# A second output bank for the second-layer products of three early two-unit slots, in a linear-attention and mixture-of-experts kernel

## The chip, the core and the metric

The kernel runs on one core of one Trainium2 chip. The metric is device time in microseconds (us) of one execution. The engines are named as in the profile: PE (TensorE, the matrix engine), PEld (its weight loads), DVE (VectorE), ACT (ScalarE), POOL (GpSimd) and SP (SyncE, which issues most of the DMA transfers). A matrix product is written into PSUM, a small memory of eight banks of 128 partitions by 512 float32 numbers, and DVE or ACT reads it from there.

## The reference

There are two parts in a row. The first is attention without softmax, for 8 batches of 8 heads with 576 tokens of 64 numbers; the second sends each of the 4608 tokens (512 numbers: 8 heads of 64) through one of 8 two-layer networks (experts).

```python
def phi(x):
    proj = np.einsum('bhsd,df->bhsf', x, w_phi)
    proj = proj - np.max(np.abs(proj), axis=-1, keepdims=True)
    return np.concatenate([np.exp(proj), np.exp(-proj)], axis=-1)
q_p, k_p = (phi(q), phi(k))
kv = np.einsum('bhsf,bhsd->bhfd', k_p, v)
z = np.sum(k_p, axis=2)
num = np.einsum('bhsf,bhfd->bhsd', q_p, kv)
den = np.einsum('bhsf,bhf->bhs', q_p, z)[..., None] + 1e-06
return (num / den).astype(np.float32)
...
logits = np.einsum('bsd,de->bse', x, w_gate)
...
    h = np.maximum(x[b, s] @ w1[e], 0.0)
    out[b, s] = p[e] * (h @ w2[e])
```

The expert `e` of a token is the largest of its eight logits, or, where a second gate says so, the expert of the token before it; `p` is the softmax of the logits.

## The kernel before

**Attention.** Work goes through the batches in four pairs. For each chunk of 128 tokens PE projects (`pj`), turns (`qt`), accumulates the key-value sums (`kvp`) and multiplies (`nm`). Its PSUM pools are `psf` (five banks), `pskv` (one bank, `kvp`) and `psb` (two banks, tag `nm`). The gate of each pair of batches gives every token an expert, and POOL writes the tokens with indirect DMAs into a list for each expert (`lst`).

**Units and slots.** In the second part the work is cut into units of 128 tokens of one expert. A slot takes one or more units through one expert's weights. A slot needs eight weight blocks of 128x1024, four for each layer. A block comes by DMA as `wraw`, ACT casts it to `whi` (line 861) and DVE takes the rest, `wlo` (line 862); every product is made of three matmuls (lines 928 to 930: `whi` and `wlo` with the high and the low part of the other operand). `layer1` writes four PSUM tiles `l1` (pool `psl`, two banks); ACT makes `hh` of each (line 963) and DVE `hl` (line 964), and the third and fourth tiles wait until the first and second have been read. `layer2` adds up 24 matmuls of 512 columns for each unit `k` in one tile `l2`; DVE scales it to `y` (line 1015), and POOL writes `y` to the output (line 1018).

**The three early slots.** Three slots of two units each run ahead of the main list of slots, right behind attention, by the call in line 144. At that time the pool `psf` has been closed and its banks belong to `psm4` (one buffer for `l2`, one for the transposes `tr`) and `psl`; `pskv` and `psb` are still open, since the last gate and the planning of the main slots use them (`pst`, tile `pt`, tag `nm`). Both units of an early slot have their `l2` in the one bank of `psm4`. Behind the third early slot `back.close()` and `open_rest` give the place of `pskv`, `psb` and attention's SBUF tiles to the pools `psr` (two buffers each for `tr` and `l2`) and `ml1` (more `wraw` buffers).

**Planning.** Between them the early slots carry the plan of the main slots: `plan_main` counts units (line 641, PE, tile `pt`; then a chain of small DVE operations from line 643), reads the token lists with indirect DMAs (`lr`, line 619), and turns them on PE (line 632, tile `pt`); DVE makes of it the token numbers `p_tokm`, with which POOL gathers the tokens (`xg`, line 889). The two steps of `plan_main` are called inside `layer2` of the first and of the second early slot, behind the first three matmuls of its second unit.

**What sets the order.** Each engine runs its instructions in one fixed order. The order is not that of the code: outside attention's loop a scheduler sets it when the kernel is built, from its own estimates of when operands and buffers are there. So a changed buffer can move instructions on every engine.

In the listings below tiles carry numbers. `l_6256` and `l_6310` are the two `l2` tiles of the first early slot, `l_6654` and `l_6684` those of the second, `l_6831` and `l_6861` those of the third; `l_6723`, `l_6750`, `l_6777` and `l_6804` are the four `l1` tiles of the third early slot, and `l_7003` and `l_7045` the first two of the first main slot.

Of the kernel before, what the change touches and what calls it, by code (L numbers as in the profile page):

```python
# [6 lines left out]
F32 = mybir.dt.float32  # L7
# [10 lines left out]
DM, E, FF = 512, 8, 1024  # L18
# [31 lines left out]
class Kernel:  # L50
# [944 lines left out]
    def layer2(self, s, gi, between, held=None):  # L995
        tc, dve, pool = self.tc, self.dve, self.pool
        hh, hl = s["h"][gi]
        u0 = s["u"] + sum(s["n"][:gi])
        for k in range(s["n"][gi]):
            self.l2n = getattr(self, "l2n", 0) + 1  # L1000
            p = self.psr if hasattr(self, "psr") and self.l2n % 3 else self.psm4
            t = p.tile([128, DM], F32, name="l2")
            o = slice(k * 128, k * 128 + 128)
            for f in range(8):
                c = slice((f % 2) * DM, (f % 2) * DM + DM)
                self.both(s, 4 + f // 2, t, hh[:, f, o], hl[:, f, o], c, f == 0, f == 7)
                if f in (0, 2) and between:
                    between.pop(0)()
                if f % 2 and gi == len(s["n"]) - 1 and k == s["n"][gi] - 1:
                    self.used(1)  # L1010
                elif f % 2:
                    self.spare()
            y = self.mx2.tile([128, DM], F32, name="yl", bufs=1) if held is not None else self.mx2.tile([128, DM], F32, name="y")
            u = u0 + k
            dve.tensor_scalar_mul(y, t, s["prob"][:, u:u + 1])  # L1015

            def put(y=y, at=s["tok"][:, u:u + 1]):
                ins = pool.indirect_dma_start(self.A["out"], bass.IndirectOffsetOnAxis(at, 0), y, None,  # L1018
                                              bounds_check=NT - 1, oob_is_err=False)
                tc.declare_no_dep(ins.ins, group="outs", reason="each token is written once")  # L1020
                tc.add_to_no_dep_group("outs", ins.ins)
            if held is None:
                put()
            else:
                held.append(put)
# [162 lines left out]
```

## Time and profile before

| | |
|---|---|
| median of 3 runs | 796.64 us (796.41 to 796.94) |
| the profiled execution: time, span | 796.07 us, 794.0 us |
| PE busy | 767.4 us (97%) |
| PEld busy | 676.2 us (85%) |
| DVE busy | 511.2 us (64%) |
| ACT busy | 401.9 us (51%) |
| POOL busy | 158.0 us (20%) |
| mean granted clock of TensorE | 0.994 of full speed |

The span is the stretch from the first to the last recorded instruction; some 2 us of the execution lie around it. Matmuls overlap, so that a busy PE is not yet a PE at its peak. The three early slots run from about 317 to 396 us of the span.

### The profile page before, as it was taken

The numbers are of one execution on the slowest core, as the hardware profiler recorded it, in microseconds if no ns is written. First come the engines' busy times: TensorE is split into PE (matmuls) and PEld (weight loads), VectorE is DVE, ScalarE is ACT, GpSimd is POOL, SyncE is SP. The second block draws the span as 40 slices with busy tenths as digits, with TensorE's granted clock in tenths as the row PEclk, the third lists the DMA queues.
The fourth block names the chain that finished last, engine by engine and source line by source line (L and its number), as shares of the span: only waits on it lengthen the run. The fifth ranks groups of instructions, "written<-read, shape, count | busy, mean of one in ns | idle before, by whom it ended". The sixth has DMA issues, their size and how long they took to land.

```text
span 794.0 us, 23193 instructions
## 1 busy us (share of the span) xinstructions
PE 767.4 (97%) x9674; PEld 676.2 (85%) x9674; DVE 511.2 (64%) x939; ACT 401.9 (51%) x708; POOL 158.0 (20%) x166
## 2 busy tenths in 40 slices
PE   6999999999999999999899999999999999999993
PEld 5899988988888989988798997698988987689882
DVE  4677798789878886985742225544866824768621
ACT  4666566666687665544531114433745713757410
POOL 0000001200275132166121102102321311110100
PEclk9999999999999999999999999999999999999997
DMA  7655454454687721747922695733966679959300
GB/s 200 195 163 155 116 146 128 135 139 122 172 264 208 223 77 42 225 148 277 333 83 88 261 347 180 258 120 114 362 204 201 244 262 410 358 188 321 111 27 14
DMA packets 77227, 151.29 MB, mean 191 GB/s; under 512 B 8524, under 2 KB 50828, under 8 KB 77078
## 3 DMA queue, kind: packets, MB, share of 16 engines
q1 hardware_dynamic: 67424, 127.33, 49.6%
q0 software_dynamic: 7424, 20.08, 7.1%
q10 hardware_dynamic: 2272, 2.37, 0.9%
q8 instruction: 77, 1.26, 0.7%
q14 instruction: 30, 0.25, 0.1%
HBM read 128.21 MB, written 22.06 MB: 189 GB/s over the span
## 4 chain that ended last, share of the span: by engine, by line
PE 84%; DVE 5%; DMA 4%; issue 2%; ACT 1%; SPq 1%; another core or an unknown queue 0%; POOLq 0%; POOL 0%; DVEq 0%
PE l L928 15%; PE l L930 15%; PE l L929 15%; PE kvp L255 9%; PE nm L314 9%; PE pj L213 9%; PE qt L233 4%; PE l L941 4%; DMA wraw<-in_w1h 3%; PE tr L914 2%; DVE m L216 1%; PE nm L293 1%; DVE sb L218 1%; PE nm L281 1%; PE tr L980 1%
## 5 line engine op out<-in xcount | busy, mean ns | idle before, releaser
L861 ACT CAST whi<-wraw 128x1024 fp32r<-128x1024 f32 x136 | 142.2, 1048 | 155.9 <-PE l L930 68.9
L862 DVE TENSOR_TENSOR wlo<-wraw,whi 128x1024 fp32r<-128x1024 f32 x128 | 156.2, 1222 | 75.4 <-ACT whi L861 73.7
L928 PE MATMUL l<-xhi,whi 128*128 128x256 f32 x512 | 146.2, 285 | 1.0 <-DVE hl L964 1.0
L930 PE MATMUL l<-xhi,wlo 128*128 128x256 f32 x512 | 143.7, 281 | 0.0
L929 PE MATMUL l<-xlo,whi 128*128 128x256 f32 x512 | 143.6, 281 | 0.0
L216 DVE TENSOR_REDUCE m<-pj 128x8 f32<-128x1024 f32 x72 | 87.8, 1220 | 47.4 <-PE pj L213 46.8
L928 PE MATMUL l<-whi,hh 128*128 128x512 f32 x288 | 114.5, 398 | 2.7 <-DVE y L1015 1.7
L930 PE MATMUL l<-whi,hl 128*128 128x512 f32 x288 | 113.2, 393 | 0.6 <-DVE hl L964 0.6
L929 PE MATMUL l<-wlo,hh 128*128 128x512 f32 x288 | 112.7, 391 | 0.0
L236 ACT ACTIVATE qp<-qt 128x512 f32<-128x512 f32 x144 | 84.7, 604 | 52.5 <-PE qt L233 52.0
L222 ACT ACTIVATE kp<-sb 128x512 f32<-128x512 f32 x144 | 82.8, 622 | 50.4 <-DVE sb L218 44.1
L928 PEld LDWEIGHTS l<-xhi,whi 128*128 128x128 f32 x512 | 96.8, 189 | 3.5 <-DVE hl L964 1.5
L929 PEld LDWEIGHTS l<-xlo,whi 128*128 128x128 f32 x512 | 96.8, 189 | 0.4
L930 PEld LDWEIGHTS l<-xhi,wlo 128*128 128x128 f32 x512 | 96.9, 189 | 0.1
L213 PE MATMUL pj<-first,kq 64*128 64x128 f32 x1152 | 85.5, 289 | 6.8 <-DMA kq<-in_kqT 6.8
L218 DVE TENSOR_TENSOR sb<-pj,m 128x1024 f32<-128x1024 f32 x72 | 88.1, 1224 | 4.0
L1018 POOL DMA_INDIRECT out<-y,p_tokm x31 | 39.2, 1263 | 244.2 <-DVE y L1015 243.6
L314 PE MATMUL nm<-kvs,qp 128*64 128x74 f32 x2304 | 86.7, 228 | 0.3
L213 PEld LDWEIGHTS pj<-first,kq 64*128 64x128 f32 x1152 | 71.5, 191 | 12.1 <-issue 4.6
L314 PEld LDWEIGHTS nm<-kvs,qp 128*64 128x64 f32 x2304 | 79.3, 136 | 1.4 <-ACT kvs L295 0.5
L255 PE MATMUL kvp<-v,kp 128*64 128x65 f32 x2048 | 77.3, 225 | 0.0
L255 PEld LDWEIGHTS kvp<-v,kp 128*64 128x64 f32 x2048 | 67.7, 139 | 5.9 <-issue 5.7
(229 smaller groups left out, 1028.1 us busy)
## 6 DMA issues: line engine op xcount, KB each, us to landing
wraw<-in_w1h SPq DMA_DIRECT2D x68, 512.0 KB, 5.3
wraw<-in_w2h SPq DMA_DIRECT2D x68, 512.0 KB, 5.1
kq<-in_kqT SPq DMA_DIRECT2D x47, 384.0 KB, 3.9
v<-in_va SPq DMA_DIRECT2D x48, 195.0 KB, 3.7
xs<-xo SPq DMA_DIRECT2D x48, 128.0 KB, 2.4
whi<-in_w1h SPq DMA_DIRECT2D x8, 512.0 KB, 4.3
wlo<-in_w1h SPq DMA_DIRECT2D x8, 512.0 KB, 5.0
whi<-in_w2h SPq DMA_DIRECT2D x8, 512.0 KB, 10.4
```

What stands on the lines that cost most here:

```text
L213: self.last_pe = self.pe.matmul(t[:, h, i % 2, j, :], kq[r, j, s], self.w2[r], start=True, stop=True)
L216: dve.tensor_reduce(m, f, AX.X, ALU.max, apply_absolute_value=True)
L218: self.last_dve = dve.tensor_sub(sb.rearrange("p h c j f -> p (h c j) f"), f, m.unsqueeze(2).broadcast_to([128, 8, 128]))
L222: self.last_act = act.activation(kp[:, :, :, sg, :].rearrange("p c h f -> p h c f"), sb[:, :, :, 0], AF.Exp, scale=1.0 - 2 * sg)
L236: self.act.activation(qp[:, sg], t, AF.Exp, scale=1.0 - 2 * sg)
L255: self.pe.matmul(self.kvp[r, sg, h], self.ch[i]["kp"][:, h, sg, r], self.v(i, b)[:, h], start=first and n < 2, stop=last and n >= 6)
L314: self.pe.matmul(e["t"][r, c - c0, h, :], self.ch[i]["qp"][:, sg, h, q0 + r.start:q0 + r.stop], kvs[:, sg, h, :], start=sg == 0, stop=sg == 1)
L861: self.act.copy(hi, raw)
L862: (low or self.dve).tensor_sub(lo, raw, hi.bitcast(F32))
L928: mm(o, ah, bh, start=first, stop=False)
L929: mm(o, ah, bl, start=False, stop=False)
L930: self.last_pe = mm(o, al, bh, start=False, stop=last)
```

## The change

In `layer2`, as long as `psr` does not exist (that is, in the early slots alone), the first unit (`k` is 0) keeps the bank of `psm4`, and the second unit takes one of the two banks of `psb` by the tag `nm`. In the main slots the choice between `psr` and `psm4` stays.

```diff
             self.l2n = getattr(self, "l2n", 0) + 1
-            p = self.psr if hasattr(self, "psr") and self.l2n % 3 else self.psm4
-            t = p.tile([128, DM], F32, name="l2")
+            if hasattr(self, "psr"):
+                p, kw = self.psr if self.l2n % 3 else self.psm4, {}
+            else:
+
+                p, kw = (self.psb, dict(tag="nm")) if k else (self.psm4, {})
+            t = p.tile([128, DM], F32, name="l2", **kw)
             o = slice(k * 128, k * 128 + 128)
```

No instruction is added or taken away. The scheduler answers with other orders. On PE, in the second early slot, this is what stands before around the first matmuls of the second unit (`l_6684`), and behind them the transposes of the token lists:

```order
L930 MATMUL l_6723<-xhi,wlo 128x256
L928 MATMUL l_6723<-xhi,whi 128x256
L929 MATMUL l_6723<-xlo,whi 128x256
L928 MATMUL l_6684<-whi,hh 128x512
L929 MATMUL l_6684<-wlo,hh 128x512
L930 MATMUL l_6684<-whi,hl 128x512
L632 MATMUL pt<-first,lr 128x40 x2
```

The same place in the changed kernel:

```order
L928 MATMUL l_6654<-whi,hh 128x512
L929 MATMUL l_6654<-wlo,hh 128x512
L930 MATMUL l_6654<-whi,hl 128x512
L928 MATMUL l_6684<-whi,hh 128x512
L929 MATMUL l_6684<-wlo,hh 128x512
L930 MATMUL l_6684<-whi,hl 128x512
L632 MATMUL pt<-first,lr 128x40 x2
```

Eleven matmuls of the next slot's first layer (`l_6723`) stood between the two units; they now come behind the second unit. In the first early slot eight such matmuls move in the same way.

On ACT, in the third early slot, this stands before, from the first weight cast for the first main slot (`whi_6955`) on:

```order
L861 CAST whi_6955<-wraw_6953 128x1024
L861 CAST whi_6961<-wraw_6959 128x1024
L963 ACTIVATE hh_6721<-l1_6723 128x512
L861 CAST whi_6967<-wraw_6965 128x1024
L861 CAST whi_6973<-wraw_6971 128x1024
L963 ACTIVATE hh_6721<-l1_6750 128x512
L861 CAST whi_6979<-wraw_6977 128x1024
L861 CAST whi_6985<-wraw_6983 128x1024
L963 ACTIVATE hh_6721<-l1_6777 128x512
```

The same place in the changed kernel:

```order
L861 CAST whi_6955<-wraw_6953 128x1024
L861 CAST whi_6961<-wraw_6959 128x1024
L861 CAST whi_6967<-wraw_6965 128x1024
L963 ACTIVATE hh_6721<-l1_6723 128x512
L861 CAST whi_6973<-wraw_6971 128x1024
L861 CAST whi_6979<-wraw_6977 128x1024
L963 ACTIVATE hh_6721<-l1_6750 128x512
L861 CAST whi_6985<-wraw_6983 128x1024
L861 CAST whi_6991<-wraw_6989 128x1024
L963 ACTIVATE hh_6721<-l1_6777 128x512
```

Each of the three `hh` now stands behind one weight cast more; on DVE `hl` and `wlo` have changed places in the same way.

On PE, at the end of the third early slot, the first unit is followed by the second, where eight transposes of the first main slot's tokens stood between:

```order
 L929 MATMUL l_6831<-wlo,hh 128x512
 L930 MATMUL l_6831<-whi,hl 128x512
-L914 MATMUL tr<-first,xg 128x128 x8
 L928 MATMUL l_6861<-whi,hh 128x512
 L929 MATMUL l_6861<-wlo,hh 128x512
```

Behind the second unit the first main slot begins:

```order
 L929 MATMUL l_6861<-wlo,hh 128x512
 L930 MATMUL l_6861<-whi,hl 128x512
-L914 MATMUL tr<-first,xg 128x128 x8
+L914 MATMUL tr<-first,xg 128x128 x14
 L928 MATMUL l_7003<-xhi,whi 128x256
+L928 MATMUL l_7045<-xhi,whi 128x256
+L914 MATMUL tr<-first,xg 128x128 x6
 L929 MATMUL l_7003<-xlo,whi 128x256
 L930 MATMUL l_7003<-xhi,wlo 128x256
```

Twenty transposes now stand there, where eight stood: the eight that were between the units, the eight that were here, and four (of a later tile) from further on. Four of the twenty write into a buffer of `psr` that lies on the bank of `l_6861`, and so wait for its `y`; the last four wait for the `xlo` that DVE makes of those. ACT casts all four token tiles (`xhi`) behind the fifth weight cast there, where two came ahead of four of the casts.

## Rows read from the trace of the kernel before

**Rows 1.** The page, busy time of each engine

```profile
PE 767.4 (97%) x9674; PEld 676.2 (85%) x9674; DVE 511.2 (64%) x939; ACT 401.9 (51%) x708; POOL 158.0 (20%) x166
```

**Rows 2.** Windows 397 to 781 us: sum of busy times (x)

```profile
sum 384.00, PE 383.99 PEld 333.37 DVE 198.62 ACT 160.10 POOL 67.04; mean PE 96.00 PEld 83.34 DVE 49.65 ACT 40.03 POOL 16.76
```

**Rows 3.** Waits of PE, 310 to 445 us: total, times, longest

```profile
PE l L928 <- DVE y L1015: 1.7, 2, 1.2
PE l L928 <- DVE hl L964: 1.0, 1, 1.0
PE l L928 <- DVE p_rim L607: 0.9, 1, 0.9
```

**Rows 4.** Timeline of PE, first and second slot: start, us

```profile
338.22 0.21 PE L641 MATMUL pt<-cnt,consts 128*36 128x8 bf16 x2
...
361.29 0.28 PE L928 MATMUL l<-xhi,whi 128*128 128x256 f32 x1
...
363.96 0.50 PE L928 MATMUL l<-whi,hh 128*128 128x512 f32 x1 [1.21 <-DVE y L1015]
...
364.85 0.41 PE L632 MATMUL pt<-first,lr 40*128 40x40 f32 x2
...
370.13 0.28 PE L930 MATMUL l<-xhi,wlo 128*128 128x256 f32 x1
```

**Rows 5.** Timeline of DVE, first and second slot

```profile
338.44 0.23 DVE L643 TENSOR_SCALAR p_um<-pt 36x8 int32<-36x8 f32 x2 [1.17 <-PE pt L641]
...
362.02 1.22 DVE L862 TENSOR_TENSOR wlo<-wraw,whi 128x1024 fp32r<-128x1024 f32 x1 [0.87 <-ACT whi L861]
363.16 0.74 DVE L1015 TENSOR_SCALAR y<-l,p_probe 128x512 f32<-128x512 f32 x1
```

**Rows 6.** Waits of SP's DMA queue, 356 to 366 us

```profile
SPq L851 <- PE pt L632: 2.0, 1, 2.0
SPq L851 <- DVE wlo L862: 1.2, 1, 1.2
SPq L851 <- DMA lr<-lst,p_rim: 1.0, 1, 1.0
```

**Rows 7.** The list's DMAs, 330 to 372 us: issue to landing

```profile
DMA to landing us min/median/max: 2.1/2.3/6.0
```

**Rows 8.** Timeline of PE, third slot and what follows

```profile
378.43 0.38 PE L928 MATMUL l<-xhi,whi 128*128 128x256 f32 x1 [0.95 <-DVE hl L964]
...
381.40 0.39 PE L928 MATMUL l<-whi,hh 128*128 128x512 f32 x1
...
387.15 0.50 PE L930 MATMUL l<-whi,hl 128*128 128x512 f32 x1 [0.63 <-DVE hl L964]
...
388.19 1.03 PE L914 MATMUL tr<-first,xg 128*128 128x128 f32 x8
389.75 0.51 PE L928 MATMUL l<-whi,hh 128*128 128x512 f32 x1 [0.53 <-DVE y L1015]
...
395.42 1.03 PE L914 MATMUL tr<-first,xg 128*128 128x128 f32 x8
396.20 0.37 PE L928 MATMUL l<-xhi,whi 128*128 128x256 f32 x1
```

**Rows 9.** Timeline of ACT, third slot

```profile
378.34 1.05 ACT L861 CAST whi<-wraw 128x1024 fp32r<-128x1024 f32 x1 [1.34 <-DMA wraw<-in_w2h]
...
395.66 1.05 ACT L861 CAST whi<-wraw 128x1024 fp32r<-128x1024 f32 x1 [0.33 <-PE l L930]
396.61 1.06 ACT L923 CAST xhi<-tr 128x512 fp32r<-128x512 f32 x2
```

**Rows 10.** Timeline of DVE, third slot

```profile
377.68 0.69 DVE L964 SCALAR_TENSOR_TENSOR hl<-l,hh 128x512 fp32r<-128x512 f32 x1
...
396.51 0.75 DVE L1015 TENSOR_SCALAR y<-l,p_probf 128x512 f32<-128x512 f32 x1
397.22 1.29 DVE L924 TENSOR_TENSOR xlo<-tr,xhi 128x512 fp32r<-128x512 f32 x2
```

## The prediction

> **What bounds the kernel now.** I read the page's busy times first: PE has work for 97% of the span [rows 1], so time is won only where PE stands still. The windows behind the early slots show PE without a gap up to its end: 383.99 of 384 us [rows 2]. What moves the first main slot's start therefore moves the end by as much, and all that counts is when PE begins there, at 396.20 in the trace [rows 8]. Third, the waits of PE around the early slots. They are few, and they name what the change is about: twice 1.7 us together for `y`, once 0.9 us [rows 3]. That one is put down to `p_rim`, but its matmul is the first of `l_6654`, which needs the bank that `y` of the unit before it still reads; `p_rim` only stands next to `y` on DVE. The timelines give the two of `y`: 1.21 us at 363.96 [rows 4] and 0.53 us at 389.75 [rows 8]. So 0.90 + 1.21 + 0.53 = 2.64 us of PE's time lie in waits for one bank, and 1.6 us more in waits for `hl` in the third slot [rows 8]. I make the sum against the profiled execution's 796.07 us; the median of the runs is 0.57 us above it, and I put the difference found on top of the median.
>
> **What the change does, part by part.** It adds and removes no instruction. It removes waits and moves work, so I follow PE from slot to slot.
>
> *First early slot.* The eight matmuls that PE does before while `y` is made cover that wait entirely; nothing is won on PE. But the counting matmuls (`pt`, line 641) come earlier, as eight matmuls no longer stand ahead of them. DVE waits 1.17 us for them and starts its planning chain at 338.44 [rows 5]. In the new order the second of the two has to wait until DVE has read the first, so not all of that is won: I take 0.7 us for the chain. Then the 0.90 us wait goes too, and PE reaches the second unit of the second slot, `l_6684`, some 0.5 us ahead of 361.29 [rows 4], say at 360.8.
>
> *Second early slot.* Before, PE does eleven matmuls from 361.29, waits for `y` until 363.96, does three of `l_6684`, and then the transposes of the list (line 632) at 364.85 [rows 4]. `y` was late because DVE had a `wlo` of 1.22 us ahead of it [rows 5]. Now the three matmuls run at once and the transposes are due at 361.5. They need the list read (`lr`), though. SP's queue waits for three things in a row ahead of its next load: 1.0 for the list read, 1.2 for `wlo`, 2.0 for the transposes [rows 6]. Counted back from the end of the transposes (364.85 + 0.41, about 365.25), the list was there at about 362.05. POOL issues it behind the list's writes, which the change doesn't move; so I leave that time as it is, and the new wait is the list read, about 0.6 us. The transposes then run at 362.15, which is 2.7 us earlier, and SP's loads of the first main slot's weights follow them.
>
> PE itself wins less there. Twenty-one matmuls at 0.23 us and then the eleven bring it to where it was at 370.13 [rows 4] by about 368.8.
>
> *Third early slot.* What PE waits for here is `hl` of the second `l1` tile, until 378.43 [rows 8]; DVE makes it at 377.68 [rows 10]. In the new order one weight block more stands ahead of it on ACT and on DVE: the one that is cast at 378.34, when its DMA had landed [rows 9]. If its landing came 2.7 us earlier, as the loads' start does, the cast would begin at 375.6 and take 1.05, `wlo` 1.22 behind it, `hl` 0.69: 378.5, and no time is won. If POOL's gathers, which start less than SP's loads do ahead of time, leave the loads more of the DMA engines, I put the landing 4 us earlier at most, and `hl` is there at 377.3. So the last `l1` tile begins at 377.3 to 378.5 against 378.43; I take the middle, **-0.5 us**.
>
> From there to the end of the second unit the trace has 395.42 - 378.43 = 16.99 us [rows 8]. The last `l1` tile takes 381.40 - 378.43 = 2.97 of it; a unit without waits takes 395.42 - 389.75 = 5.67, with a slow first matmul behind its wait, and I take 5.6. Without the two waits and without the transposes between: 2.97 + 2 x 5.6 = 14.17. That is **-2.8 us**. I cost the wait for `hl` inside the unit (0.63 at 387.15 [rows 8]) at nothing, since the loads ahead of it are at least 2.7 us earlier; if that cover is gone it is back whole.
>
> *Start of the main slots.* Call the end of `l_6861` T (before: 395.42). Before, eight transposes follow and the first main matmul stands at T + 0.78 [rows 8]. Now the first tile's tokens are still to be turned, and one of the buffers is the bank that `y` of `l_6861` reads. The trace has this `y` at 396.51, T + 1.1, since a `wlo` that PE itself released stands ahead of it, and the next operation at T + 1.8 [rows 10]. So: `y` is read at T + 1.85; four transposes, to T + 2.4; ACT's cast to T + 3.1 (the last weight cast ahead of it starts at T + 0.24 [rows 9] and is done by then); the first main matmul at T + 3.2. On DVE meanwhile one `xlo` (0.64, half of the 1.29 at 397.22 [rows 10]) to T + 2.45, one `wlo` of 1.2 to T + 3.6, the `xlo` of the late tile to T + 4.25; the last four transposes wait for it and end at T + 4.7, and only then does PE go on without gaps. Of this, four transposes (0.4) and two matmuls (0.23) are work pulled forward from later. So 4.7 - 0.63 - 0.78: **+3.3 us**.
>
> Here a page's rule speaks for the change. Perfetto Trace Analysis in the Trainium skill, "Optimizing Tensor Performance", says that independent groups of matmuls should go through different PSUM banks, so that one is read out while the next is multiplied. By it alone the 2.64 us are won; the new wait on the same two banks, a step later, is outside what it weighs.
>
> *Sum.* -0.5 - 2.8 + 3.3 = 0.0 us: 796.07 stays 796.1 for the profiled execution, and 796.6 beside the median. Its parts are large, their sum is not; bounds: -1.1 to +0.1, -2.9 to -2.2 (with the wait for `hl` back), +2.2 (if `y` were not behind the `wlo`, 1.1 less) to +3.8 (if that `wlo`'s load lands 0.5 late). Together -1.8 to +1.7.
>
> **The rivals.**
>
> *The waits for the bank simply go.* The new orders cost nothing, 2.64 us are won: 794.0 us. For it: the waits are there, and PE is the bound everywhere else. Against it: the transposes that now wait for the second unit's `y` had nothing to wait for before, and DVE puts that `y` behind a `wlo`. It needs PE going on without gaps by about T + 3.1, 1.6 us less than my T + 4.7.
>
> *The list read comes later still.* The planning and the weight loads of the second slot start 0.7 us earlier and share the DMA engines with the list's writes and reads, whose landings already spread from 2.1 to 6.0 us [rows 7]. PE stands at the transposes for as long as the list is late, and the loads behind them too. A microsecond costs one; with 2.0 us the last `l1` tile of the third slot begins at about 380, and the time is 798.6 us. From 1.6 us on it is slower. For it: there is no spare time at this place any more, where there were 2.8 us (362.05 to 364.85). Against it: the writes themselves are issued as before.
>
> *Nothing comes of it because everything goes by DMA.* The chain through the third slot is loads, casts and `wlo`; if it alone set the start of the main slots, they would follow SP's loads and begin 2 us earlier, 794.6 us. Against it: from T on, PE, DVE and ACT wait for one another, not for loads.
>
> **How the numbers follow.** About 0.2% (1.6 us) is what a measurement of this kernel can tell from no change. My forecast, gains and losses that cancel, gets 0.60; the waits that simply go 0.14 and the DMA chain 0.08, both faster by over 1.6 us; the late list read 0.18. My forecast's own bounds (-1.8 and +1.7) pass 1.6 us by so little that I leave its 0.60 whole under "same", and add 0.02 of the late list read, for lists late by less than 1.6 us. That gives 0.22 faster, 0.62 same, 0.16 slower. The predicted time is 796.6 us. The range goes from 794.4, which takes in the DMA chain and most of the way to the first rival, to 798.6, the late list read.
>
> **What would show it right or wrong.** In the profile after: no matmul of PE waits for `y` of a first unit; PE stands still ahead of line 632 at about 361.5 and goes on when the list has landed; SP's loads of the main slots start near 362.7, where they stood behind the transposes at about 365.3; the last `l1` tile of the third slot still waits for `hl`, now for 1 to 2 us; behind `l_6861` there is a gap on PE, in two or three pieces with transposes between, and from T to the second main matmul some 4.7 us; behind it PE has no gap, as before. The prediction is wrong if PE stands still for under 1 us in all behind `l_6861` (then faster), if the list read lands after 363.7 (then slower), or if PE meets a new wait in the main slots.

## The result and the profile after

The change makes the kernel slower: 799.54 us median (796.71 to 801.49, 12 runs) against 796.94 us beside it (793.63 to 798.10, 12 runs), a ratio of 1.0035 with a 95% interval of 1.0023 to 1.0046, or +2.8 us (1.8 to 3.7). The profiled execution took 800.73 us with a span of 798.7 us and a mean granted clock of 0.989. It is one of the slower of the 12: 4.7 us above the profiled execution before, where the medians differ by 2.6.

The page's busy times, which answer to [rows 1], show the same work in a longer span:

```profile
PE 770.0 (96%) x9674; PEld 678.5 (85%) x9674; DVE 511.6 (64%) x939; ACT 401.6 (50%) x708; POOL 159.2 (20%) x166
```

The window from 405 to 786 us is as full as in [rows 2], so what is lost is lost before 405 us:

```profile
405.00:786.00 381.00, 380.99 (x2479) 330.23 (x2477) 196.08 (x224) 158.94 (x227) 63.36 (x53) 1.00 0.60 213
```

The waits of PE from 300 to 786 us, against [rows 3]. No second-layer product waits for `y` any more; in its place the list's transposes (line 632) wait 4.3 us for their DMA, and the first main transposes (line 914) wait for `y` and `xlo`:

```profile
PE pt L632 <- DMA lr<-lst,p_rim: 4.3, 1, 4.3
PE tr L914 <- DVE y L1019: 1.2, 1, 1.2
PE l L928 <- DVE hl L964: 1.1, 3, 0.5
PE tr L914 <- DVE xlo L924: 0.3, 1, 0.3
```

The timeline of PE through the second and third slot, which answers to [rows 4, 8]:

```profile
365.50 0.44 PE L632 MATMUL pt<-first,lr 40*128 40x40 f32 x2 [4.34 <-DMA lr<-lst,p_rim]
365.88 0.80 PE L928 MATMUL l<-whi,hh 128*128 128x512 f32 x1
366.47 0.63 PE L929 MATMUL l<-wlo,hh 128*128 128x512 f32 x1
...
371.99 0.40 PE L930 MATMUL l<-whi,hl 128*128 128x512 f32 x1
...
382.76 0.39 PE L928 MATMUL l<-xhi,whi 128*128 128x256 f32 x1 [0.49 <-DVE hl L964]
...
385.73 0.39 PE L928 MATMUL l<-whi,hh 128*128 128x512 f32 x1
...
396.86 0.60 PE L914 MATMUL tr<-first,xg 128*128 128x128 f32 x4
398.70 1.31 PE L914 MATMUL tr<-first,xg 128*128 128x128 f32 x10 [1.24 <-DVE y L1019]
...
401.10 0.66 PE L914 MATMUL tr<-first,xg 128*128 128x128 f32 x4 [0.34 <-DVE xlo L924]
401.51 0.36 PE L929 MATMUL l<-xlo,whi 128*128 128x256 f32 x1
```

Three things are to be seen. The transposes of the list run at 365.50, not at the forecast 362.15. The 13 matmuls from 366.47 to 371.99 take 0.425 us each, where those behind take 0.23: 2.5 us more. And the start of the main slots stands as forecast: T is 396.86, PE goes on at T + 4.65 (forecast T + 4.7), and from the last `l1` tile at 382.76 to T it is 14.10 us (forecast 14.17, before 16.99).

Windows of all engines (PE's busy time first; the granted clock is the number before the last two) behind that wait. PE stands still at a clock of 1.00, works at 0.50, which is 1.2 GHz, for some 6 us, and is then back at 1.00, 2.4 GHz:

```profile
362.00:365.00 3.00, 0.00 (x0) 0.00 (x0) 1.38 (x2) 0.00 (x0) 1.02 (x1) 1.00 0.31 85
366.00:371.00 5.00, 5.00 (x12) 3.94 (x13) 0.34 (x3) 1.05 (x1) 3.62 (x4) 0.50 0.75 251
372.00:380.00 8.00, 8.00 (x63) 7.69 (x62) 5.11 (x6) 2.95 (x5) 3.69 (x3) 1.00 1.00 372
```

The trace alone tells a simple story, theory A: the list came late, and its wait and the half clock behind it cost the 2.8 us. Theory B puts the loss at the third slot: it doesn't get back the 3.3 us that the start of the main slots costs. Theory C says that the new first slot makes the list itself later.

### The profile page after: what moved, and what is told of

Same layout as the page of the kernel before. It is cut to its first block, busy times and chain, and to the rows that moved or that the text cites. A ratio compares the mean times of both kernels' runs of the same rounds, so it can differ in the third digit from the quotient of the medians.

```text
span 798.7 us, 23193 instructions
## 1 busy us (share of the span) xinstructions
PE 770.0 (96%) x9674; PEld 678.5 (85%) x9674; DVE 511.6 (64%) x939; ACT 401.6 (50%) x708; POOL 159.2 (20%) x166
## 4 chain that ended last, share of the span: by engine, by line
PE 84%; DVE 5%; DMA 3%; issue 2%; ACT 1%; SPq 1%; POOL 0%; another core or an unknown queue 0%; POOLq 0%; DVEq 0%
PE l L928 15%; PE l L929 15%; PE l L930 15%; PE kvp L255 9%; PE nm L314 9%; PE pj L213 9%; PE qt L233 4%; PE l L941 4%; PE tr L914 2%; DMA wraw<-in_w2h 1%; DVE m L216 1%; PE nm L293 1%; DVE sb L218 1%; PE nm L281 1%; DMA lr<-lst,p_rim 1%
## 5 line engine op out<-in xcount | busy, mean ns | idle before, releaser
L964 DVE SCALAR_TENSOR_TENSOR hl<-l,hh 128x512 fp32r<-128x512 f32 x64 | 43.9, 687 | 45.6 <-ACT hh L963 45.6
```

## The experiments

All change the same line, or a few beside it. The early slots are named `e0`, `e1` and `f0` in the code. The runs fell on several chips of two kinds: on some the kernel before takes 796.3 to 796.9 us, on the others 809.5 to 810.4. On the second kind the list has landed long before its transposes, so they tell the wait from the rest. Differences are worked out from the ratio and the time of before beside it; each comes from 12 runs, those of the filled wait from 6.

| kernel | before, us | ratio (95%) | us (95%) |
|---|---|---|---|
| the change | 796.94 | 1.0035 (1.0023 to 1.0046) | +2.8 (1.8 to 3.7) |
| the change, a2 | 810.44 | 1.0030 (1.0017 to 1.0043) | +2.4 (1.4 to 3.5) |
| the change, a3 | 810.39 | 1.0019 (1.0003 to 1.0036) | +1.5 (0.2 to 2.9) |
| e1, first slot | 809.50 | 1.0000 (0.9986 to 1.0013) | 0.0 (-1.1 to 1.1) |
| e2, second slot | 809.50 | 0.9986 (0.9973 to 0.9999) | -1.1 (-2.2 to -0.1) |
| e2b, second slot | 796.32 | 0.9995 (0.9982 to 1.0009) | -0.4 (-1.4 to 0.7) |
| e3, third slot | 809.50 | 1.0018 (1.0002 to 1.0034) | +1.5 (0.2 to 2.8) |
| e3b, third slot | 796.32 | 1.0014 (1.0002 to 1.0025) | +1.1 (0.2 to 2.0) |
| e12, first and second | 796.32 | 1.0005 (0.9988 to 1.0023) | +0.4 (-1.0 to 1.8) |
| e12b, first and second | 809.97 | 0.9984 (0.9969 to 0.9999) | -1.3 (-2.5 to -0.1) |
| e5, third swapped | 809.50 | 1.0005 (0.9995 to 1.0015) | +0.4 (-0.4 to 1.2) |
| e14, second, third swapped | 796.32 | 1.0005 (0.9992 to 1.0018) | +0.4 (-0.6 to 1.4) |
| e6, change, late list | 810.44 | 1.0011 (0.9995 to 1.0027) | +0.9 (-0.4 to 2.2) |
| e6r, change, late list | 810.39 | 1.0009 (0.9995 to 1.0023) | +0.7 (-0.4 to 1.9) |
| e15, e12 with late list | 810.39 | 0.9985 (0.9969 to 1.0000) | -1.2 (-2.5 to 0.0) |
| e15b, e12 with late list | 809.97 | 0.9990 (0.9973 to 1.0006) | -0.8 (-2.2 to 0.5) |
| e7, change, filled wait | 810.44 | 1.0089 (1.0069 to 1.0108) | +7.2 (5.6 to 8.8) |
| e7r, change, filled wait | 810.39 | 1.0103 (1.0082 to 1.0124) | +8.3 (6.6 to 10.0) |

The traces begin up to some microseconds apart, so I compare them from the first second-layer matmul of the first early slot (before: 330.08). Three points stand in this table: that zero, the first second-layer matmul of the third slot, and the first of the main slots, ahead of which every kernel has done the same work. The last column is the stretch between the last two.

| trace | zero at | third slot's second layer | main slots' second layer | between |
|---|---|---|---|---|
| before | 330.08 | 51.32 | 89.71 | 38.39 |
| third slot (e3b) | 330.25 | 51.30 | 90.87 | 39.57 |
| second slot (e2b) | 329.37 | 54.14 | 90.76 | 36.62 |
| first and second (e12) | 329.63 | 54.34 | 90.95 | 36.61 |
| the change | 329.02 | 56.71 | 95.39 | 38.68 |
| before, 810 us (b2) | 334.46 | 62.56 | 100.20 | 37.64 |
| first slot, 810 us (e1) | 333.44 | 60.00 | 97.99 | 37.99 |
| second slot, 810 us (e2) | 332.29 | 59.23 | 97.08 | 37.85 |
| third slot, 810 us (e3) | 334.06 | 60.32 | 101.01 | 40.69 |
| first and second, 810 us (e12b) | 334.40 | 62.94 | 99.54 | 36.60 |
| the change, 810 us (a2) | 335.54 | 61.02 | 100.31 | 39.29 |
| the change, 810 us (a3) | 333.33 | 62.78 | 102.40 | 39.62 |

On the second kind of chip the third column differs by 2.2 us between b2 and e3, where before and e3b on the first kind agree within 0.02, so the traces there are best compared by the last column.

**One slot at a time.** The first slot (e1), the second (e2, e2b) and the third (e3, e3b) have the new bank alone.

```diff
-                p, kw = (self.psb, dict(tag="nm")) if k else (self.psm4, {})
+                p, kw = (self.psb, dict(tag="nm")) if k and s["name"] == "e0" else (self.psm4, {})
```

In the other two `"e0"` reads `"e1"` or `"f0"`.

> Only the first early slot's second unit has its products in attention's bank; the second and third slot stay as before. Theory A (the loss is the list read's wait at the second slot, 4.3 us in the trace of the change, and the half clock behind it, about 2.8 us): within 0.5 us of before, 796.4 to 797.4, and the transposes of the list wait no longer than in the trace before. Theory B (the loss is the start of the main slots, +3.3 us): the same. Theory C (this slot delays GpSimd's scatters, so that the list lands 2 us later than before in any case): 1 to 2 us slower, with a wait of the transposes for the list.

> Only the second early slot's second unit has its products in attention's bank. Theory A: slower than before by 2 to 5.5 us, with a wait of the list's transposes for the read of 2 to 5 us, and TensorE's granted clock at its half behind that wait for some 6 us. Theory B: 1.2 us faster than before, since only the wait of that unit for the first unit's y (1.21 us) goes.

> Only the third early slot's second unit has its products in attention's bank. Theory A: within 0.5 us of before plus 0.4: the 2.9 us that fall away between the two units come back as 3.3 us at the first transposes of the main slots, which wait for the second unit's y (1.2 us) and xlo (0.3 us). Theory B: 2 to 3.3 us slower.

> The second slot alone, again. On a chip of about 810 us before: -1.1 again, within 1. On one of about 797 us: theory A +2 to +5.5 with a wait for the list of 2 us or more; theory B -1.2.

> The third slot alone, again. On a chip of about 810 us before: +1.5 again, within 1 (between the units 1 to 2 us fall away, 3.3 come at the start of the main slots). On one of about 797 us: +0.4, since 2.9 fall away there.

The first slot does nothing on the chips where the list is there; on the other kind it was not run alone. The second is faster by 1.1 us where the list is there, and is not slower where it isn't, though its trace has the wait that theory A blames. The third is slower on both kinds of chip, though e3 by less than theory B's 2 to 3.3. The rows of e2b at the transposes, and the windows around them:

```profile
363.34 0.41 PE L632 MATMUL pt<-first,lr 40*128 40x40 f32 x2 [2.14 <-DMA lr<-lst,p_rim]
```
```profile
361.00:363.00 2.00, 0.20 (x1) 0.00 (x0) 0.80 (x1) 1.04 (x1) 0.00 (x0) 1.00 0.25 82
364.00:369.00 5.00, 5.00 (x25) 4.14 (x24) 0.60 (x4) 1.05 (x1) 3.71 (x4) 1.00 0.82 264
```

PE waits 2.14 us and the clock stays at 1.00. The third slot's second layer begins 2.8 us later than before, but 1.8 us of that come back ahead of the main slots (38.39 against 36.62), though nothing was changed there. The trace keeps a loss of 1.0 us, which the runs' -0.4 (-1.4 to 0.7) don't show. Theory A has the wait right and its price wrong.

The rows of e3b show what the third slot gains and pays. From 381.55 to T at 393.57 it is 12.02 us instead of 14.02 [rows 8], and PE goes on at T + 4.65 instead of T + 0.78:

```profile
381.55 0.39 PE L928 MATMUL l<-whi,hh 128*128 128x512 f32 x1
...
393.57 0.60 PE L914 MATMUL tr<-first,xg 128*128 128x128 f32 x4
395.40 1.31 PE L914 MATMUL tr<-first,xg 128*128 128x128 f32 x10 [1.24 <-DVE y L1019]
...
397.81 0.66 PE L914 MATMUL tr<-first,xg 128*128 128x128 f32 x4 [0.34 <-DVE xlo L924]
398.22 0.36 PE L929 MATMUL l<-xlo,whi 128*128 128x256 f32 x1
```

That is -2.0 and, with the 0.63 us of work pulled forward, +3.24: +1.2, the table's 39.57 against 38.39, and the +1.1 of the runs. That is theory B; my expectation of +0.4 counted on 2.9 us where 2.0 fell away.

**The first two slots together, and the change again.** e12 and e12b have the condition `k and s["name"] != "f0"`; a2 and a3 are the change itself. b2 is the kernel before, for its trace on the second kind of chip; it took 810.87 us.

> The change itself once more, beside a trace of the kernel before on the same chip. If this chip takes about 797 us before: 1.5 to 4.5 us slower, and the list's transposes wait 2 to 5 us (theory A), or they don't wait and the loss stands at the start of the main slots (theory B). If it takes about 809 us before, as the chip of the first four experiments did, where the list is asked for early and lands some 10 us before its transposes: no wait for the list, so the sum of the second slot's -1.1 and the third slot's +1.5, about 0.4 us slower.

> The kernel before, for its trace on this chip: the time of the before runs beside it, within their spread.

> The change in the first and second early slot, the third as before. Theory B (what the change loses on every chip is the third slot, about 1.5 us, and the second slot gains 1.1 where the list is there): 1.1 us faster than before on a chip where the list is there before its transposes (before at about 810 us); on a chip where the transposes wait for the list (before at about 797 us) 2 to 5 us slower by theory A. Theory D (the parts add up to more than their sum, 2.4 against 0.4, because the first and the second slot together hurt): 0.5 to 1 us slower than before on either chip.

> The change itself, beside the three. On a chip of about 797 us: +2.8 again within 1, with a wait for the list of 3 us or more and the half clock behind it, and 11.1 to 12 us from the third slot's first second-layer product to the end of those products. On a chip of about 810 us: +2.4 again, within 1.

> The change in the first two slots, the third as before, again. On a chip of about 810 us: if the third slot is what the change loses by there (1.5 us alone, change 1.6 to 2.0 over before), 0 to 1 us faster than before; if the first two slots hurt together, slower. On a chip of about 797 us: within 1 us of before again, with a wait for the list of 2 us or more.

On the 810 us chips the change is slower too, by 2.4 and 1.5 us, and its list's transposes don't wait at all (a3):

```profile
376.42 0.41 PE L632 MATMUL pt<-first,lr 40*128 40x40 f32 x2
...
396.11 0.39 PE L928 MATMUL l<-whi,hh 128*128 128x512 f32 x1
...
407.24 0.60 PE L914 MATMUL tr<-first,xg 128*128 128x128 f32 x4
409.07 1.31 PE L914 MATMUL tr<-first,xg 128*128 128x128 f32 x10 [1.24 <-DVE y L1019]
```

So the list's wait is not what the change loses by there, and my expectation of a2, +0.4 by the sum of the parts, missed by 2 us. Without the third slot the runs show no loss on either kind: +0.4 and -1.3. The third slot in the company of the other two then costs 2.8 - 0.4 = 2.4 us on one kind and, with a2 and a3, 2.8 to 3.7 on the other, where alone it cost 1.1 and 1.5. Each of these differences has an interval of over 1.5 us to either side, so the runs alone don't show that it costs more in company.

On the first kind the table's last column does: 38.68 - 36.61 = 2.1 in company, 39.57 - 38.39 = 1.2 alone. On the second it does not: 39.29 and 39.62 against 36.60 are 2.7 and 3.0 in company, and e3's 40.69 is 2.7 to 3.1 above b2, e1 and e2, whose third slot is the old one.

Why it is more in company on the first kind is seen in e12's third slot, which has the old order and the old bank. PE's rows, and behind them DVE's of before and of e12 around the first unit's `y`:

```profile
383.97 0.39 PE L928 MATMUL l<-whi,hh 128*128 128x512 f32 x1
...
389.52 1.04 PE L914 MATMUL tr<-first,xg 128*128 128x128 f32 x8
390.53 0.50 PE L928 MATMUL l<-whi,hh 128*128 128x512 f32 x1
...
396.20 1.03 PE L914 MATMUL tr<-first,xg 128*128 128x128 f32 x8
```
```profile
387.81 1.22 DVE L862 TENSOR_TENSOR wlo<-wraw,whi 128x1024 fp32r<-128x1024 f32 x1 [0.71 <-ACT whi L861]
388.95 0.74 DVE L1015 TENSOR_SCALAR y<-l,p_probf 128x512 f32<-128x512 f32 x1
```
```profile
387.53 1.23 DVE L862 TENSOR_TENSOR wlo<-wraw,whi 128x1024 fp32r<-128x1024 f32 x1 [0.30 <-ACT whi L861]
389.72 0.75 DVE L1019 TENSOR_SCALAR y<-l,p_probf 128x512 f32<-128x512 f32 x1 [0.97 <-PE l L930]
```

The `wlo` ahead of `y` runs at nearly the same time in both, 57.7 and 57.9 us behind the zero, though the third slot began 3.0 us later in e12: it waits for ACT's cast, and that cast had waited for its load (1.00 and 0.88 us). In the trace before, PE is done with the first unit at 388.19 [rows 8] and `y` is late behind it. In e12 PE is done at 389.52, DVE is free and waits for PE, and nobody waits for `y` or for `hl`: the stretch takes 12.23 us by itself, where it took 14.02. Of the 2.9 us that the change seems to win there, 1.8 had gone already; the rest, 1.1 us, is nearly all the eight transposes (1.0), which only move behind T. On the second kind the stretch from the third slot's second layer to T takes 13.27 us in b2, 13.61 in e1 and 13.47 in e2, 12.22 in e12b, 12.31 in e3 and 11.12 and 11.13 in a2 and a3.

**The third slot with its banks swapped.** e5 swaps them in the third slot alone; e14 has the second slot's change too. The main transposes then find attention's bank free early.

```diff
+                p, kw = (self.psb, dict(tag="nm")) if not k and s["name"] == "f0" else (self.psm4, {})
```

> Only the third early slot is changed, with the two banks the other way round: the first unit in attention's bank and the second in the bank that both used, so that the first transposes of the main slots find attention's bank free. Theories A and B both: the 2.9 us between the units fall away and the 3.3 us at the start of the main slots don't come, 793.5 to 794.5, with no wait of the transposes for y. If another wait (xlo, or hl of the slot itself) takes the place of that one, no less than 796.

> The second slot as in the change, the third with the two banks the other way round, the first as before. By the runs so far on the chips of about 810 us (second alone -1.1, third swapped -0.4 to +0.4): 0.7 to 1.5 us faster than before. On a chip of about 797 us: the swapped third gives -1.5 to -2.9 and the second's list wait +2 to +5.4, so 0 to 3.5 us slower by theory A, and 2 to 4 us faster if the list is not what costs.

By its ratio e5 loses 0.4 us where e3 lost 1.5, though the intervals overlap, and no gain comes. In e5 no transpose waits for `y`, but all sixteen still stand behind T, and the first matmul waits for ACT's cast of them:

```profile
405.93 1.47 PE L914 MATMUL tr<-first,xg 128*128 128x128 f32 x12
408.20 0.51 PE L928 MATMUL l<-xhi,whi 128*128 128x256 f32 x2 [0.80 <-ACT xhi L923]
```

So of the expected 2.9 us nothing shows. On the other kind of chip e14's +0.4 stands against e2b's -0.4, again without a gain; its transposes waited 1.55 us for the list, again at a clock of 1.00.

**The list's transposes later, and the wait filled.** In e6, e6r, e15 and e15b the transposes stand behind the seventh of the second unit's eight steps (of `f`), where they stood behind its first.

```diff
-                if f in (0, 2) and between:
+                if f in (0, 2, 4, 6) and between:
...
-later=[[no, no, more]] * 2)
+later=[[no] * 4 + [more], [no] * 7 + [more]])
```

> The change, with the two transposes of the list four steps later in the second slot's second unit (behind its seventh f instead of its first), some 4 us of products later. Theory A on a chip with the list wait: the wait of 4.3 us falls under 0.5, no half clock, and the time is 3 to 5 us under the change's, so 1 us under before or equal to it; the loads behind the list on SyncE start no earlier, which may give back up to 2 us. Theory B: no different from the change. On a chip without the list wait: no different from the change, or up to 1 us slower by the later list.

> The change in the first and second slot, with the list's transposes four steps later in the second unit; the third slot as before. Theory E (what the second slot loses or gains is mostly taken up by the third slot's waits between its units, 14.02 us from its first product to the end of its products in the trace of before and 12.23 when it comes 3.0 us later): no wait for the list, no half clock, and still within 0.8 us of before. Theory A alone (the list's wait is what the second slot costs, and without it the 1.2 us of the wait for y are won): 1 to 2 us faster than before. Theory F (the loads of the main slots' weights stand behind the list on SyncE, and come 4 us later): 1 to 4 us slower, with new waits of TensorE for hl or weights in the third slot.

> The whole change with the list's transposes four steps later, again. On a chip of about 797 us, theory E: no wait for the list, between before and the change, about 0.5 to 1.5 us slower than before, since the third slot still pays 3.2 us at the start of the main slots and gets 2 to 2.9 back. Theory A alone: 1 us faster than before to equal. On a chip of about 810 us: 0.9 us slower again, within 1.

> The change in the first two slots with the list's transposes four steps later, again. On a chip of about 797 us: no wait for the list, no half clock; theory F (the third slot's hh and hl stand in ScalarE's and VectorE's queues behind the casts of the weights whose loads start at the list's transposes) 1 us slower than before to equal, with TensorE's waits for hl in the third slot longer than the 1.6 us in the trace of before; theory A alone 1 to 2 us faster. On a chip of about 810 us: 1.2 us faster again, within 1.

All four met chips on which the list doesn't wait, so what the later place gives back where it does was not measured. What they show is that little hangs on the place there: e6 is 1.5 us under a2, e6r 0.8 under a3, and e15b 0.5 over e12b, all within their intervals. Theory F, loads behind the list that come too late, is not seen in the times. In the traces of e15 and e15b PE does wait in the third slot, 0.4 to 0.5 us for `hl` inside the first unit and 0.9 for `y`, where e12b's has neither wait; whether the later loads do that was not followed. In e7 and e7r the transposes stay where the change has them, and 18 matmuls that the reference does not need stand ahead of them (`self.hh` is the second slot's `hh`):

```diff
+        if name == "m":
+            ft = self.psm4.tile([128, 4, 128], F32, name="tr").rearrange("p a b -> p (a b)")
+            for _ in range(18):
+                with self.tc.issue_after(self.last_pe.ins):
+                    self.last_pe = self.pe.matmul(ft, self.hh[:, 0, 0:128], self.hh[:, 0:2, :], start=True, stop=True)
...
+            self.hh = hh
```

> The change, with 18 products of 512 columns into a bank that nobody reads, put ahead of the list's transposes, so that TensorE is busy for the 4.1 us of the wait (18 x 0.23) and the wait itself stays. They are work beyond the reference's and their result is dropped. Theory A, with the half clock as a cost of its own: the granted clock stays at its full level behind the list, and the time is 2 to 2.8 us under the change's. If the clock costs nothing beside the wait: the change's time within 0.5. On a chip without the list wait: 4 us slower than the change, all of them on TensorE's path.

> The change with 18 products beyond the reference's ahead of the list's transposes (4.1 us of work whose result is dropped), again. On a chip of about 797 us: the granted clock stays at its full level behind the list; if the half clock costs what the rows show (1.6 to 2.8 us in the traces with a wait of 3.1 and 4.3 us), 0.5 to 2.8 us faster than the change; if it costs nothing of its own, no faster, or up to 1 us slower since the 4.1 us of work are longer than a short wait. On a chip of about 810 us: 5 us slower than the change again.

These too met no wait, and so price extra work instead of the clock. The row of e7, and the window of the third slot behind it:

```profile
375.79 4.29 PE L631 MATMUL tr<-hh 128*128 128x512 f32 x18
```
```profile
384.00:404.00 20.00, 16.36 (x106) 15.56 (x105) 12.23 (x13) 10.38 (x13) 5.40 (x5) 0.83 1.01 388
```

Against the change on the same chip they cost 5.2 us (817.55 - 812.39) and 6.9 us (818.76 - 811.88), more than the 4.3 of the row: in the window PE stands still for 3.6 of 20 us and the clock falls to 0.83 in the mean. In a2's window at the same place it stands still for 2.1 us at a full clock:

```profile
381.00:401.00 20.00, 17.94 (x124) 16.40 (x123) 12.94 (x14) 11.36 (x13) 7.38 (x6) 1.00 1.01 398
```

What makes the longer wait was not followed further.

## Why the prediction was wrong

What failed stands ahead of T: I had -0.5 and -2.8 us there, with a list that is late by 0.6 us only. The runs show about 0 for the first two slots, and in the traces the third slot behind them gains 1.1 us instead of 2.8. The +3.3 us of the start of the main slots came as forecast.

**First slot.** Nothing on PE, as forecast: e1 is at 0.0. The 0.7 us for the planning chain did not help the list. These are the issues of its read by POOL, before and in the change:

```profile
358.48 1.31 POOL L619 DMA_INDIRECT lr<-lst,p_rim  x1 [0.31 <-issue]
```
```profile
359.64 1.55 POOL L619 DMA_INDIRECT lr<-lst,p_rim  x1 [0.31 <-issue]
```

They stand 28.4 and 30.6 us behind the zero; in e2b it is 28.8, in e12 30.0: with the first slot changed two of POOL's indirect DMAs ahead of it take 1.7 to 1.9 us to issue, where before and in e2b they take 0.9 to 1.4. That agrees with theory C, in one trace each; why they do is open.

**Second slot.** This step failed. I put the list's landing at 362.05, counted back from a row of SP's waits [rows 6] as if the list's wait stood ahead of the one for `wlo`. It stood behind it: asked of 356 to 362.2 us the same view has the wait for `wlo` alone, and asked of 363.3 to 366 us the one for the transposes alone. So the list landed about 363.25 (365.25 - 2.0), 33.2 us behind the zero, and the spare time was 1.6 us, not 2.8. In e2b SP's wait for the list ends between 363.3 and 363.4 and PE is released at 363.34, which bears this reading out. Nor did the landing stay where it was, as I had assumed: it came 34.0 us behind the zero in e2b, 35.0 in e12 and 36.5 in the change, where it is 365.50 and so behind the 363.7 that I had named as the point from which the forecast is wrong. Of the 3.3 us in the change 2.2 are the later issue, and the rest a longer way from issue to landing (5.86 against 4.77 us). So PE arrived at the third slot 2.8 to 5.4 us late in three traces, where I had it 0.5 us early. The rival that priced this, the list read later at 798.6 us, was nearest to the result, but not for its reason alone: in e2b and e12 the third slot gave 1.8 of some 3 us back, and the runs of these two were not slower.

**Third slot, between the units: -2.8.** This step failed with it. The size was right against the trace before (14.10 us, forecast 14.17) and wrong as a gain. It counted waits that hang on the weights' loads and on what ACT and DVE make of them, which did not move with PE (57.7 and 57.9 us behind the zero, above). With PE on time, as in e3b, 2.0 us of them went; with PE late, as the second slot made it, 1.8 had gone without the change, and the last 1.1 were work that moved.

**Start of the main slots: +3.3.** Right in place, mechanism and size on the first kind of chip: T + 4.65 in the change and in e3b, the wait for `y` 1.24 us and that for `xlo` 0.34, and from T to the main slots' second layer 27.55 us against 24.37. Behind it PE has no gap there that could give time back. On the second kind PE goes on at T + 4.65 as well, but e3, a2 and a3 meet one more wait in the first main slot, 0.55 to 0.72 us for `hl`, which no trace with the old third slot has (a2):

```profile
418.71 0.38 PE L928 MATMUL l<-xhi,whi 128*128 128x256 f32 x1 [0.72 <-DVE hl L964]
```

From T to the main slots' second layer these three take 28.2 to 28.5 us, where b2, e1, e2 and e12b take 24.4. A new wait in the main slots was among the forecast's own signs of being wrong.

**The sum.** -0.5 - 2.8 + 3.3 should have read about 0 for the first two slots (+0.4, -1.3) and +2.1 to +3.0 for the third. The trace of the change by itself reads otherwise: PE is 5.4 us late at the third slot, and from there on it loses 0.3 (38.68 against 38.39), near the forecast's -2.8 + 3.3. Only e2b and e12 tell that with the old third slot such a lateness costs little. The half clock, which the forecast did not have at all, costs 2.5 us of rows in the trace of the change and 1.4 in e12's; how much of it reached the end on chips where the list waits stays open, for e12's interval of -1.0 to +1.8 can't tell, and the runs made to price it met none of those chips. The change's own runs hint at a part: the seven with a mean granted clock of 0.989 to 0.991 took 800.3 us in the mean, the five with 0.992 to 0.994 took 798.2.

**The rule on different banks.** In the second slot the new bank is worth 1.1 us where the list is there; in the third the bank belongs to the next phase, and it costs. The rule of Perfetto Trace Analysis in the Trainium skill ("Optimizing Tensor Performance"), that independent groups of matmuls should go through different banks, was followed in all three slots.

## What to carry to other kernels

A wait that a trace shows is only a gain if whoever it waits for is ahead of the engine in the new timing as well; take it out against a kernel in which all the other parts of the change are already made. A free bank is free until its pool's next user comes: where a buffer is borrowed from one phase, look at who waits for it at the border to the next, above all if everything behind that border is already full. Run the parts alone and also all but one of them, since here the parts alone add up to 0.7 us on one kind of chip (1.1 - 0.4, and e1's 0.0 from the other kind) and to 0.4 on the other (1.5 - 1.1 + 0.0), while all three cost 2.8 on the one and 1.5 to 2.4 on the other.

## What the hardware showed that I had not expected

**The clock after a wait.** PE stood still for 1.55 us (e14) and 2.14 us (e2b) and went on at 1.00. It stood still for 3.09 us in e12 and for 4.34 us in the change, and went on at 0.50 for some 3 and some 6 us. e12's row and windows:

```profile
364.68 0.41 PE L632 MATMUL pt<-first,lr 40*128 40x40 f32 x2 [3.09 <-DMA lr<-lst,p_rim]
```
```profile
366.00:368.00 2.00, 2.00 (x6) 1.63 (x5) 0.00 (x0) 0.00 (x0) 1.54 (x2) 0.50 0.69 170
369.00:380.00 11.00, 11.00 (x84) 10.50 (x82) 7.03 (x7) 6.43 (x8) 6.14 (x5) 1.00 1.03 404
```

TensorE: Matmul & The Clock Gate in the Trainium skill, "Part 1: The HAM clock gate", says that idleness takes the clock to its lower level and activity brings it back; these rows agree.

**When an indirect read is done.** In the change's window from 356 to 366 us, in 40 slices of a quarter microsecond, the DMA engines move data up to the slice at 363.25 and then nothing until 365.25 (the numbers are GB/s):

```profile
GB/s 344 344 344 246 229 246 246 344 229 393 295 246 98 115 66 229 360 393 99 0 0 0 0 164 131 0 164 360 197 164 0 0 0 0 0 0 0 426 360 262
```

PE is released at 365.50. The data from 365.25 on, 0.26 MB up to 366 us, have the size of one `y`, whose write POOL began to issue at 363.66. If they are that write, the list's own data were done by 363.5, and PE went on 2 us or more behind the list's last byte: whoever reads this landing from the traffic is early by that much.

**Two kinds of chip.** The same kernel is 13 us slower on some chips. In the traces 9 to 11 of them lie between the zero and the third slot (60.32 in e3 and 62.56 in b2, against 51.32). In the trace of before there, DVE stands still ahead of planning operations that wait for nothing in the trace of the first kind:

```profile
353.43 0.16 DVE L728 TENSOR_TENSOR p_r<-p_r,p_pl 36x8 int32<-36x8 int32 x1 [1.75 <-remote]
355.56 0.16 DVE L649 CAST p_f<-p_r 36x8 f32<-36x8 int32 x1 [1.83 <-remote]
```

What it waits for is not recorded, and the cause is open.
